# An attention and feed-forward kernel on one core: three moves in the order of its loads, casts and fills

## The chip, the cores and the metric

The kernel runs on one core of one Trainium2 chip. The metric is the device time of one execution in microseconds (us). The kernel before the change took 229.86 us, the median of three runs (228.38, 229.86 and 230.62).

## What is computed

Two stages follow each other. The first is attention for 4 batches of 8 heads, 768 positions, head size 64. Three heads (0, 2, 6, "retrieval") look at all earlier positions; the other five ("stream") look at the first 4 positions and at a window of 64. The second stage is a feed-forward layer over the 3072 tokens, with a leaky slope of its own for each hidden unit:

```
scores = q @ k.T / sqrt(64)                  # masked: causal, or sinks and window
a = exp(scores - max) / sum
x = (a @ v) as [3072, 512]                   # heads side by side
h = x @ w_in                                 # 512 -> 2048
out = (max(h, 0) + alpha * min(h, 0)) @ w_out    # 2048 -> 512
```

All inputs are float32; the kernel works in bfloat16 with float32 sums.

## The kernel before

The heads go in pairs: (2, 6), (1, 5), (0, 4), (3, 7). With 4 batches there are 16 segments, n = 0 to 15; segment n holds pair n % 4 of batch n // 4. Segments 0 to 3 are batch 0, 4 to 7 batch 1. For each segment the kernel loads queries, keys and values, casts them to bfloat16, brings queries and keys into transposed form, multiplies keys by queries (scores), takes the exponent, multiplies by the values, divides by the sums and transposes the result into `xT`. The feed-forward layer takes a batch's 768 tokens in two groups (t even: 512 tokens, t odd: 256), multiplies them by w_in in 16 blocks of 128 hidden units and then by w_out.

Nothing decides the order at run time. A list written out by hand, `ORDER` (lines 14 to 71), names some 1,076 steps, and the kernel emits them one by one (lines 809 to 812). Each engine works through its own instructions in that order, so a step's place in the list sets what stands ahead of it on its engine and, for loads, on its queue. The names in the list that matter here:

- `Lq5`, `Lk3`, `Lv3`: the loads of segment 5's queries, segment 3's keys and values. All go out on SyncE's queue (SP). `Lq` is one DMA (line 209), `Lk` two (line 223), `Lv` two for the two heads (line 246) and, for each stream head of batch 0, one more for the last 24 rows (line 248). Four buffers each (`qf`, `kf`, `vf`) are used in turn: `Lq5` writes the buffer that `Cq1` read. SP's loads share eight semaphores in turn, so each load waits for the landing of the one eight before it.
- `Cq5`, `Ck3.0`, `Ck3.1`, `Cv2`: casts to bfloat16. Strings at lines 298 to 300 say which engine does them; for `Cq5`, `Ck3`, `Cv2` it is GpSimd (POOL). After `Cv` come small copies that repeat the first four rows for stream heads (line 308).
- `Tq5`, `tq5`: six transposes on TensorE (line 365) into a PSUM bank, and the copy out of it, here on ScalarE (line 370). `Tk`, `tk` are the same for keys.
- `S`, `s`: scores on TensorE (lines 415 and 432, masks at 464 and 503) and their exponent on ScalarE. `A`, `a`: the product with the values (line 554) and the division on VectorE. `X`, `x`: transposing the result (line 579) and copying it to `xT`.
- `wi0` to `wi7`: the loads of w_in, issued by POOL with a cast on the way (line 694). A pair, such as `wi0` and `wi1`, brings 512 of the 2048 columns. `wo0` to `wo3` are those of w_out (line 698).
- `P0.5.1`: group 0, hidden block 5, second part of the product with w_in (line 599); `p` and `g` are what ScalarE and VectorE make of it. `O`, `o`: the product with w_out (line 619) and its way out.
- `vz0` to `vz3`: VectorE fills the last slot of a value buffer with zeros (`vf[i][:, 6]`, line 710), which `Lv` then writes in part: the 24-row load of `Lv3` (line 248) waits for `vz3`. `kfz0` to `kfz3` are the same for keys on POOL (line 740).
- `warm`: TensorE products of zeros that keep it at work (line 689).

PSUM has eight banks. A step that needs one takes the one given back longest ago among those that it may use (`take`, line 144), so moving a step can change which bank it gets and whose release it waits for.

Before the change, SP's loads stand in the order Lk3, Lv1, Lq3, Lv2, Lq5, Lv3, Lk4, Lk5, Lk7, Lk6, Lq4, Lq6, and POOL's steps in the order Cv0, wi1, kfz0, Ck3.1, wi0, Ck3.0, Cq3, Cv1, Cv2, nz1, wi6, wi7, Cq5, wi5, wi4, kfz2, Cv3.0, wi2, Ck4.0, Ck4.1, kfz3, nr, Ck5.0, wi3, ns, kfz1, Ck5.1, wo0 to wo3, Cq4. Here `nz1` is a fill, `nr` and `ns` build masks.

Of the kernel before, what the change touches and what calls it, by code (L numbers as in the profile page):

```python
# [13 lines left out]
ORDER = """  # L14
busy zero La id warm0 kz3 Lq0.0 sz1 vz2 nms nmr so1 vz0 Lq0.1 Lk1 warm8 warm5 warm3 kz1 qz0 one Lq1 Lk0 Ck0.0 kz2
Cq0.0 Tq0.0 tq0.0 Tk0.0 qz warm2 Lk2 kz0 tk0.0 Ck1.0 Ck1.1 Cq0.1 Tk1 S0.0.1 s0.0.1 Tq0.1 S0.0.0 Cq1 warm7 Lv0 tk1.0
sz2 vz1 Tq1 Lq2 Ck0.1 S0.0.2 s0.0.0 tk1.1 Tk0.1 Ck2.1 tq1 S1.1.0 s0.0.2 Ck2.0 warm4 tq0.1 nz0 s1.1.0 Cq2 tk0.1 Cv0 Lk3
S0.1.0 wi1 kfz0 Lv1 vo ro0 Ck3.1 s0.1.0 Lq3 wi0 Ck3.0 Cq3 sz0 idf S1.0.0 so2 Al s1.0.0 so0 al S0.1.1 s0.1.1 Lv2 Tq2
Tk2 tk2.1 tk2.0 S0.1.2 Lq5 S1.0.1 A0.0 s0.1.2 a0.0 Cv1 A0.1 a0.1 Cv2 s1.0.1 tq2 S1.1.1 nz1 Tk3 S2.0.1 tk3.0 s1.1.1 vz3
S2.0.2 X0 s2.0.1 x0 wi6 s2.0.2 wi7 Lv3 Cq5 Tq3 tk3.1 S2.0.0 wi5 m4.0.2 warm6 S2.1.0 A1.0 a1.0 Lk4 s2.0.0 A2.0 S2.1.1  # L20
A1.1 a2.0 tq3 s2.1.0 a1.1 S3.0.0 s2.1.1 s3.0.0 A2.1 a2.1 S3.1.1 X1 S3.0.1 s3.0.1 Lk5 wi4 kfz2 Cv3.0 Lk7 wi2 X2 Tq5
Ck4.0 s3.1.1 S3.1.0 tq5 x1 P0.0.0 x2 P0.0.1 A3.0 P0.1.0 P0.1.1 Lk6 Lq4 Lq6 Ck4.1 kfz3 nr Cv3.1 s3.1.0 A3.1 Lv7 Lv5 Lq7
Ck5.0 wi3 a3.0 P0.2.0 P0.3.0 P0.3.1 a3.1 X3 x3 ns kfz1 P0.2.1 Tk4 near2 P1.2 P0.1.2 P0.2.2 P0.0.2 p1.2 p0.1 g0.1 Ck5.1
P1.0 P0.3.2 g1.2 P0.15 tk4.0 p0.2 g0.2 p0.15 wo0 p1.0 Lk8 near0 g0.15 g1.0 ro1 P1.12 P1.14 m12.1.2 p0.0 g0.0 wo1 tk4.1
p1.12 P0.14 g1.12 p0.14 g0.14 P0.13 p0.13 g0.13 P0.11 p1.14 Tk5 Ck7.1 g1.14 P1.10 tk5.0 p0.11 p1.10 Ck6.0 Ck7.0 g0.11
m8.0.2 tk5.1 wo2 Lv6 Lv4 P0.10 P0.8 p0.8 Tk7 g1.10 wo3 Cq4 Lk9 P0.12 P1.8 p0.10 g0.8 p0.12 g0.10 Tq4 P0.6 P0.9 p0.3
Ck6.1 g0.3 tq4 P0.4.0 P0.5.0 Tk6 P0.4.1 p1.8 g1.8 tk7.0 p0.9 g0.9 Cq6 P0.5.1 P0.5.2 p0.5 g0.12 p0.6 tk6.1 P0.4.2 g0.6
g0.5 tk6.0 S4.0.5 P0.7 p0.7 P1.6 g0.7 P1.4 s4.0.5 p0.4 Tq6 m4.1.2 tk7.1 g0.4 Cv5 p1.6 g1.6 O0.1.0 tq6 S4.0.3 O0.2.0
O0.2.1 S5.1.1 S5.0.0 S4.0.1 S6.1.0 m14.0.2 p1.4 g1.4 s5.0.0 O0.1.1 s4.0.3 s4.0.1 O0.2.2 S5.0.2 S5.1.0 S4.0.2 S5.1.2
s6.1.0 m4.0.1 Cv7 O0.3.0 s5.0.2 s5.1.2 s5.1.1 s4.0.2 O0.1.2 s5.1.0 O0.1.3 o0.1 Cq7 Cv4 O0.3.1 m5.1.0 m8.1.2 m5.0.2  # L30
m4.0.3 m5.1.2 S4.0.0 S4.1.4 S5.0.1 S4.0.4 S4.1.0 s4.0.4 s5.0.1 Lk10 m5.0.1 O0.2.3 O0.3.2 Tq7 m5.0.0 o0.2 s4.1.0 m4.0.4
m5.1.1 A5.1 s4.0.0 m4.0.0 a5.1 O0.3.3 tq7 S7.0.0 S7.0.1 S4.1.3 S7.1.1 S6.0.5 S4.1.1 m4.0.5 s4.1.4 o0.3 Lq9 s4.1.3 Ck8
m4.1.3 A5.0 a5.0 X5 s4.1.1 A4.0 s7.0.0 s7.1.1 Lk11 Lq8 s7.0.1 a4.0 s6.0.5 near1 m7.0.0 m7.1.1 m4.1.0 O1.1.0 S7.1.0
S6.0.4 S7.0.2 S4.1.5 S6.0.1 S7.1.2 S6.1.1 O1.1.1 Cv6 s7.1.0 O1.0.0 s4.1.5 m7.0.1 s6.1.1 m4.1.5 m6.1.1 s7.1.2 m6.1.0
s7.0.2 m7.0.2 S6.0.2 S4.1.2 S6.1.2 S6.0.0 s6.0.4 s4.1.2 s6.0.1 s6.1.2 O1.0.1 m6.0.5 m7.1.0 m4.1.1 m4.1.4 m7.1.2 m6.1.2
S6.0.3 A4.1 s6.0.0 m6.0.0 m6.0.1 A7.1 O1.1.2 A6.1 s6.0.3 m6.0.4 m6.0.3 s6.0.2 a4.1 a6.1 A6.0 A7.0 a6.0 O1.1.3 O0.0.0
O0.0.1 O0.0.2 O1.0.2 m10.0.2 O1.0.3 O0.0.3 o0.0 X4 X6 a7.1 a7.0 X7 P2.9 P2.3 p2.9 P3.4 Ck9 Cq9 g2.9 P2.14 p2.14 g2.14
Cq8 p3.4 Lq10 Lq11 Dk8.0 P2.10 p2.10 Dk9.1 o1.0 p2.3 g2.3 g3.4 Dk8.1 P3.2 P3.14 P3.12 P2.8 Dq8 P2.1 P3.8 o1.1 p3.2
Dk9.0 Lv10 g2.10 Dq9 p3.14 P2.7 Ck10 g3.2 p3.12 g3.12 g3.14 P2.2 p2.2 g2.2 Cq10 Dq10 P2.11 p2.1 g2.1 p2.11 p2.8 g2.11
P3.6 P2.5 p2.5 g2.5 P2.13 p2.13 g2.8 g2.13 P2.0 p2.0 g2.0 p2.7 P3.0 p3.0 P2.4 S8.0.5 Lv8 Lv11 P2.15 P2.12 s8.0.5 Cq11  # L40
g3.0 p2.15 g2.7 g2.15 S8.0.0 p2.12 g2.12 Ck11 p3.6 S9.0.2 P2.6 p2.6 g3.6 s8.0.0 p2.4 g2.4 g2.6 s9.0.2 p3.8 P3.10 g3.8
p3.10 O3.0.0 O2.0.0 S8.1.5 s8.1.5 O3.0.1 O2.0.1 g3.10 m8.0.0 Cv8 S8.1.3 S9.0.0 S8.0.3 S9.1.1 S8.0.1 S9.1.0 s8.1.3
s9.1.0 s8.0.1 s9.0.0 s8.0.3 m8.0.3 m8.0.1 O2.0.2 O2.0.3 o2.0 Dk10.1 Lv9 m9.0.0 Cv9 m8.0.5 Dk11.0 m9.1.0 m9.0.2 S8.0.4
S9.0.1 S10.1.1 S8.1.4 Dq11 s8.1.4 Lq13 Lk13 O3.0.2 Dk10.0 s9.1.1 s10.1.1 s9.0.1 s8.0.4 O3.0.3 o3.0 Dk11.1 S10.1.0
S10.1.2 m9.0.1 S11.0.2 S9.1.2 S8.0.2 S11.0.0 s9.1.2 Cv10 m9.1.1 A9.0 s11.0.2 s10.1.0 O2.3.0 m9.1.2 A9.1 a9.0 a9.1 X9
# [804 lines left out]
```

## Time and profile before

| what | us |
|---|---|
| median of three runs | 229.86 |
| the profiled execution | 230.9 |
| its span (first to last instruction) | 229.2 |
| TensorE busy (97% of the span) | 222.5 |
| VectorE busy | 150.6 |
| ScalarE busy | 140.8 |
| GpSimd busy | 46.0 |

The profile is one execution. Its span leaves out what lies before the first and after the last instruction, here 1.7 us. The granted TensorE clock is full in all slices of the page. The DMA engines are busy from 2 us to about 150 us; they move 37.26 MB, most of it (27.60 MB) for SP's queue and 8.93 MB for POOL's. The start of the program, until 28 us, is attention for batch 0 alone; from 28.07 us on TensorE also multiplies by w_in. Times in the text count from the span's start.

### The profile page before, as it was taken

The page shows a single profiled execution, that of the slowest core. Times are in us where ns is not written, and L with a number is a line of the kernel's source. Part 1 is how long each engine was busy: PE and PEld are TensorE (multiplying, and loading weights), DVE is VectorE, ACT ScalarE, POOL GpSimd, SP SyncE. Part 2 cuts the span into 40 slices and gives each one's busy share as a digit, 9 for nine tenths or more (in the row PEclk, how much of TensorE's full clock was granted, in tenths as well). Part 3 has the DMA queues.
Part 4 walks back from the last instruction along what each step waited for, and adds up shares of the span by engine and source line. Part 5 has one row for each costly group of instructions (what it writes and reads, how often), then busy time and mean ns, then how long its engine had stood idle before and what let it go on. Part 6 is the DMA issues. An engine that isn't in the chain of part 4 may idle for free.

```text
span 229.2 us, 5248 instructions
## 1 busy us (share of the span) xinstructions
PE 222.5 (97%) x2005; PEld 136.1 (59%) x2005; DVE 150.6 (66%) x394; ACT 140.8 (61%) x285; POOL 46.0 (20%) x91
## 2 busy tenths in 40 slices
PE   8997999999999999999999999999999999999994
PEld 8887966654455656555456455556556555664454
DVE  5779749975479915899699209986586635966000
ACT  3889529999799127477995127787594236563311
POOL 6775998100230001000400001000110110000000
PEclk9999999999999999999999999999999999999999
DMA  6999999999997799999969799995821420000213
GB/s 196 307 231 214 249 228 270 206 196 210 212 264 166 131 198 215 191 149 193 247 167 216 174 272 152 204 185 99 138 93 38 115 94 0 0 4 0 92 72 112
DMA packets 94957, 37.26 MB, mean 163 GB/s; under 512 B 81980, under 2 KB 93140, under 8 KB 94932
## 3 DMA queue, kind: packets, MB, share of 16 engines
q1 hardware_dynamic: 88676, 27.60, 60.9%
q0 software_dynamic: 5792, 8.93, 17.7%
q10 hardware_dynamic: 464, 0.40, 0.5%
q8 instruction: 15, 0.25, 0.5%
q14 instruction: 10, 0.08, 0.1%
HBM read 27.58 MB, written 6.29 MB: 148 GB/s over the span
## 4 chain that ended last, share of the span: by engine, by line
PE 87%; DMA 3%; ACT 3%; DVE 3%; SPq 1%; issue 1%; POOL 0%; DVEq 0%; POOLq 0%
PE P L599 35%; PE P L619 33%; PE P L554 7%; PE P L432 4%; DMA vf<-in_v_dram 3%; PE P L689 3%; PE P L638 2%; ACT neg L604 1%; PE P L365 1%; DVE kT L394 1%; PE P L579 1%; DVE eS L530 1%; PE P L425 1%; ACT kT L394 1%; PE P L415 1%
## 5 line engine op out<-in xcount | busy, mean ns | idle before, releaser
L611 DVE SCALAR_TENSOR_TENSOR g<-neg,oma,P 128x256 bf16<-128x256 f32 (+1 forms) x128 | 71.0, 608 | 36.1 <-ACT neg L604 35.6
L599 PE MATMUL P<-xT,w_in_b 128*128 128x512 bf16 (+1 forms) x512 | 86.3, 326 | 0.0
L619 PE MATMUL P<-w_out_b,g 128*128 128x512 bf16 x368 | 85.4, 379 | 0.0
L604 ACT ACTIVATE neg<-P 128x512 f32<-128x512 f32 x96 | 54.1, 599 | 29.5 <-PE P L599 25.1
L599 PEld LDWEIGHTS <-w_in_b 128*128 128x128 bf16 x512 | 49.5, 98 | 31.9 <-DVE g L611 0.2
L619 PEld LDWEIGHTS <-g 128*128 128x128 bf16 x368 | 33.7, 98 | 37.3 <-issue 1.2
L471 ACT ACTIVATE eR<-P 128x448 bf16<-128x448 f32 (+4 forms) x63 | 37.0, 634 | 5.4 <-PE P L432 2.5
L625 ACT COPY ot<-P 128x512 f32<-128x512 f32 x23 | 13.8, 601 | 37.7 <-PE P L619 32.9
L629 POOL DMA_DIRECT2D out_dram<-ot x18 | 10.3, 571 | 112.9 <-ACT ot L625 112.7
L519 ACT ACTIVATE eS<-P 128x352 bf16<-128x352 f32 x45 | 20.9, 491 | 3.7 <-PE P L432 3.7
L565 DVE TENSOR_TENSOR xn<-P,rcp 128x448 bf16<-128x448 f32 (+1 forms) x32 | 19.4, 608 | 1.1
L530 DVE TENSOR_TENSOR eS<-eS,ms_near 128x352 bf16<-128x352 bf16 x45 | 15.0, 351 | 4.4 <-ACT eS L519 4.2
L481 DVE TENSOR_TENSOR eR<-eR,mr_near 128x128 bf16<-128x128 bf16 (+5 forms) x54 | 10.7, 225 | 4.0 <-ACT eR L471 4.0
L432 PE MATMUL P<-qT,kT 64*128 64x176 bf16 (+13 forms) x181 | 11.7, 251 | 0.3 <-DVE g L611 0.3
L564 DVE RECIPROCAL rcp<-P 128x7 f32<-128x7 f32 (+1 forms) x32 | 6.3, 197 | 8.5 <-PE P L554 8.4
L432 PEld LDWEIGHTS <-kT 64*128 64x128 bf16 x181 | 7.2, 94 | 7.6 <-issue 6.4
L415 PE MATMUL P<-qT,kT 128*128 128x192 bf16 (+14 forms) x68 | 11.3, 251 | 0.2 <-ACT eS L525 0.2
L554 PE MATMUL P<-vb,eS 128*128 128x65 bf16 x260 | 11.0, 193 | 0.4 <-DVE eS L530 0.4
L554 PEld LDWEIGHTS <-eS 128*128 128x128 bf16 x260 | 9.7, 97 | 2.9 <-DVE eS L530 0.6
L554 PE MATMUL P<-vb,eR 128*128 128x65 bf16 x276 | 10.1, 193 | 1.2 <-POOL vb L350 1.2
L554 PEld LDWEIGHTS <-eR 128*128 128x128 bf16 x276 | 9.5, 97 | 2.4 <-issue 1.3
L647 DVE COPY ot<-P 128x128 f32<-128x128 f32 x1 | 0.3, 292 | 14.3 <-PE P L638 14.3
(96 smaller groups left out, 177.4 us busy)
## 6 DMA issues: line engine op xcount, KB each, us to landing
out_dram<-ot POOLq DMA_DIRECT2D x18, 256.0 KB, 3.6
kf<-in_k_dram SPq DMA_DIRECT2D x21, 192.0 KB
qf<-in_q_dram SPq DMA_DIRECT2D x18, 192.0 KB
vf<-in_v_dram SPq DMA_DIRECT2D x17, 192.0 KB
vf<-in_v_dram SPq DMA_DIRECT2D x14, 196.0 KB
qf<-in_q_dram SPq DMA_DIRECT2D x7, 384.0 KB
w_in_b<-in_moe_w_in_dram POOLq DMA_DIRECT2D x8, 256.0 KB, 9.0
w_out_b<-in_moe_w_out_dram POOLq DMA_DIRECT2D x4, 512.0 KB, 13.4
```

The lines of the kernel that those rows point to most:

```text
L415: nc.tensor.matmul(to, keys, queries, start=True, stop=stop)
L432: nc.tensor.matmul(to, keys[own], queries[own], start=True, stop=True)
L471: nc.scalar.activation(ebuf[n, hh][:, lo:hi].rearrange("p (x c) -> p x c", x=len(parts)), P[:, got[0]:got[0] + len(parts), 0:(hi - lo) // ...
L519: nc.scalar.activation(slots, sc[:, 0:352].rearrange("p (s c) -> p s c", c=176), AF.Exp, scale=scale)
L530: nc.vector.tensor_tensor(slots, slots, ms_near[:, 0:2, :] if m == 0 else ms_near[:, 1:3, :], op=ALU.mult)
L554: nc.tensor.matmul(pav[:, i, :], e[:, o:o + 128], vv[:, j, hh, 0:D + 1], start=(m == 0), stop=(m == len(terms) - 1))
L565: nc.vector.tensor_tensor(xn[n][:, 0:nt, D * hh:D * hh + D], pav[:, :, 0:D], rcp.to_broadcast([128, nt, D]), op=ALU.mult)
L599: nc.tensor.matmul(psg[:, w * i:w * (i + 1)], w_in_b[:, c, 128 * fb:128 * (fb + 1)], xT[:, c, o:o + w], start=(x == 0), stop=(x == 3))
L604: nc.scalar.activation(neg[t, f], bank(held["P", t, f][0]), AF.Relu, scale=-1.0)
L611: nc.vector.scalar_tensor_tensor(g_buf[t % 2][:, fb, 0:w], neg[t, f][:, c], oma[:, fb:fb + 1], bank(got[0])[:, c], op0=ALU.mult, op1=ALU.add)
L619: nc.tensor.matmul(bank(held["O", t, s][0]), g_buf[t % 2][:, f, 128 * s:128 * (s + 1)], w_out_b[:, f, :], start=(f == 0), stop=(f == 15))
L625: nc.scalar.copy(ot, bank(got[0]))
```

## The change

Only `ORDER` changes. Four things move, and no step is added or removed:

- `wi1` and `wi0`, the first two loads of w_in on POOL, go behind `Ck3.1` and `Ck3.0`, the casts of the last pair's keys. POOL's order becomes Cv0, kfz0, Ck3.1, Ck3.0, wi1, wi0, Cq3.
- `vz3`, a fill on VectorE, goes from ahead of `x0` to right behind `vz1`, ahead of `tk1.1`.
- `Lq5`, the load of batch 1's second pair of queries, goes on SP's queue from ahead of `Lv3` to behind it.
- What follows from that load goes later too: `Cq5` on POOL from ahead of wi5 to behind Cv3.0, `Tq5` on TensorE and `tq5` on ScalarE from ahead of `S3.1.0` (Tq5) and right behind it (tq5) to behind `P0.1.1`.

The lines of the list that differ in more than where they break, from line 17 on, with those after:

```diff
-sz2 vz1 Tq1 Lq2 Ck0.1 S0.0.2 s0.0.0 tk1.1 Tk0.1 Ck2.1 tq1 S1.1.0 s0.0.2 Ck2.0 warm4 tq0.1 nz0 s1.1.0 Cq2 tk0.1 Cv0 Lk3
-S0.1.0 wi1 kfz0 Lv1 vo ro0 Ck3.1 s0.1.0 Lq3 wi0 Ck3.0 Cq3 sz0 idf S1.0.0 so2 Al s1.0.0 so0 al S0.1.1 s0.1.1 Lv2 Tq2
-Tk2 tk2.1 tk2.0 S0.1.2 Lq5 S1.0.1 A0.0 s0.1.2 a0.0 Cv1 A0.1 a0.1 Cv2 s1.0.1 tq2 S1.1.1 nz1 Tk3 S2.0.1 tk3.0 s1.1.1 vz3
-S2.0.2 X0 s2.0.1 x0 wi6 s2.0.2 wi7 Lv3 Cq5 Tq3 tk3.1 S2.0.0 wi5 m4.0.2 warm6 S2.1.0 A1.0 a1.0 Lk4 s2.0.0 A2.0 S2.1.1
-A1.1 a2.0 tq3 s2.1.0 a1.1 S3.0.0 s2.1.1 s3.0.0 A2.1 a2.1 S3.1.1 X1 S3.0.1 s3.0.1 Lk5 wi4 kfz2 Cv3.0 Lk7 wi2 X2 Tq5
-Ck4.0 s3.1.1 S3.1.0 tq5 x1 P0.0.0 x2 P0.0.1 A3.0 P0.1.0 P0.1.1 Lk6 Lq4 Lq6 Ck4.1 kfz3 nr Cv3.1 s3.1.0 A3.1 Lv7 Lv5 Lq7
...
+sz2 vz1 vz3 Tq1 Lq2 Ck0.1 S0.0.2 s0.0.0 tk1.1 Tk0.1 Ck2.1 tq1 S1.1.0 s0.0.2 Ck2.0 warm4 tq0.1 nz0 s1.1.0 Cq2 tk0.1 Cv0
+Lk3 S0.1.0 kfz0 Lv1 vo ro0 Ck3.1 s0.1.0 Lq3 Ck3.0 wi1 wi0 Cq3 sz0 idf S1.0.0 so2 Al s1.0.0 so0 al S0.1.1 s0.1.1 Lv2
+Tq2 Tk2 tk2.1 tk2.0 S0.1.2 S1.0.1 A0.0 s0.1.2 a0.0 Cv1 A0.1 a0.1 Cv2 s1.0.1 tq2 S1.1.1 nz1 Tk3 S2.0.1 tk3.0 s1.1.1
+S2.0.2 X0 s2.0.1 x0 wi6 s2.0.2 wi7 Lv3 Lq5 Tq3 tk3.1 S2.0.0 wi5 m4.0.2 warm6 S2.1.0 A1.0 a1.0 Lk4 s2.0.0 A2.0 S2.1.1
+A1.1 a2.0 tq3 s2.1.0 a1.1 S3.0.0 s2.1.1 s3.0.0 A2.1 a2.1 S3.1.1 X1 S3.0.1 s3.0.1 Lk5 wi4 kfz2 Cv3.0 Cq5 Lk7 wi2 X2
+Ck4.0 s3.1.1 S3.1.0 x1 P0.0.0 x2 P0.0.1 A3.0 P0.1.0 P0.1.1 Tq5 tq5 Lk6 Lq4 Lq6 Ck4.1 kfz3 nr Cv3.1 s3.1.0 A3.1 Lv7 Lv5
...
```

More of the change, by code (lines that the diff above doesn't have):

```diff
@@ L21 @@
-A1.1 a2.0 tq3 s2.1.0 a1.1 S3.0.0 s2.1.1 s3.0.0 A2.1 a2.1 S3.1.1 X1 S3.0.1 s3.0.1 Lk5 wi4 kfz2 Cv3.0 Lk7 wi2 X2 Tq5
-Ck4.0 s3.1.1 S3.1.0 tq5 x1 P0.0.0 x2 P0.0.1 A3.0 P0.1.0 P0.1.1 Lk6 Lq4 Lq6 Ck4.1 kfz3 nr Cv3.1 s3.1.0 A3.1 Lv7 Lv5 Lq7
-Ck5.0 wi3 a3.0 P0.2.0 P0.3.0 P0.3.1 a3.1 X3 x3 ns kfz1 P0.2.1 Tk4 near2 P1.2 P0.1.2 P0.2.2 P0.0.2 p1.2 p0.1 g0.1 Ck5.1
-P1.0 P0.3.2 g1.2 P0.15 tk4.0 p0.2 g0.2 p0.15 wo0 p1.0 Lk8 near0 g0.15 g1.0 ro1 P1.12 P1.14 m12.1.2 p0.0 g0.0 wo1 tk4.1
-p1.12 P0.14 g1.12 p0.14 g0.14 P0.13 p0.13 g0.13 P0.11 p1.14 Tk5 Ck7.1 g1.14 P1.10 tk5.0 p0.11 p1.10 Ck6.0 Ck7.0 g0.11
@@ L26 @@
[L26 to L40, printed above, removed]
@@ L41 @@
-g3.0 p2.15 g2.7 g2.15 S8.0.0 p2.12 g2.12 Ck11 p3.6 S9.0.2 P2.6 p2.6 g3.6 s8.0.0 p2.4 g2.4 g2.6 s9.0.2 p3.8 P3.10 g3.8
-p3.10 O3.0.0 O2.0.0 S8.1.5 s8.1.5 O3.0.1 O2.0.1 g3.10 m8.0.0 Cv8 S8.1.3 S9.0.0 S8.0.3 S9.1.1 S8.0.1 S9.1.0 s8.1.3
+sz2 vz1 vz3 Tq1 Lq2 Ck0.1 S0.0.2 s0.0.0 tk1.1 Tk0.1 Ck2.1 tq1 S1.1.0 s0.0.2 Ck2.0 warm4 tq0.1 nz0 s1.1.0 Cq2 tk0.1 Cv0
+Lk3 S0.1.0 kfz0 Lv1 vo ro0 Ck3.1 s0.1.0 Lq3 Ck3.0 wi1 wi0 Cq3 sz0 idf S1.0.0 so2 Al s1.0.0 so0 al S0.1.1 s0.1.1 Lv2
+Tq2 Tk2 tk2.1 tk2.0 S0.1.2 S1.0.1 A0.0 s0.1.2 a0.0 Cv1 A0.1 a0.1 Cv2 s1.0.1 tq2 S1.1.1 nz1 Tk3 S2.0.1 tk3.0 s1.1.1
@@ new lines @@
+S2.0.2 X0 s2.0.1 x0 wi6 s2.0.2 wi7 Lv3 Lq5 Tq3 tk3.1 S2.0.0 wi5 m4.0.2 warm6 S2.1.0 A1.0 a1.0 Lk4 s2.0.0 A2.0 S2.1.1
+A1.1 a2.0 tq3 s2.1.0 a1.1 S3.0.0 s2.1.1 s3.0.0 A2.1 a2.1 S3.1.1 X1 S3.0.1 s3.0.1 Lk5 wi4 kfz2 Cv3.0 Cq5 Lk7 wi2 X2
+Ck4.0 s3.1.1 S3.1.0 x1 P0.0.0 x2 P0.0.1 A3.0 P0.1.0 P0.1.1 Tq5 tq5 Lk6 Lq4 Lq6 Ck4.1 kfz3 nr Cv3.1 s3.1.0 A3.1 Lv7 Lv5
+Lq7 Ck5.0 wi3 a3.0 P0.2.0 P0.3.0 P0.3.1 a3.1 X3 x3 ns kfz1 P0.2.1 Tk4 near2 P1.2 P0.1.2 P0.2.2 P0.0.2 p1.2 p0.1 g0.1
+Ck5.1 P1.0 P0.3.2 g1.2 P0.15 tk4.0 p0.2 g0.2 p0.15 wo0 p1.0 Lk8 near0 g0.15 g1.0 ro1 P1.12 P1.14 m12.1.2 p0.0 g0.0 wo1
@@ new lines @@
+tk4.1 p1.12 P0.14 g1.12 p0.14 g0.14 P0.13 p0.13 g0.13 P0.11 p1.14 Tk5 Ck7.1 g1.14 P1.10 tk5.0 p0.11 p1.10 Ck6.0 Ck7.0
+g0.11 m8.0.2 tk5.1 wo2 Lv6 Lv4 P0.10 P0.8 p0.8 Tk7 g1.10 wo3 Cq4 Lk9 P0.12 P1.8 p0.10 g0.8 p0.12 g0.10 Tq4 P0.6 P0.9
+p0.3 Ck6.1 g0.3 tq4 P0.4.0 P0.5.0 Tk6 P0.4.1 p1.8 g1.8 tk7.0 p0.9 g0.9 Cq6 P0.5.1 P0.5.2 p0.5 g0.12 p0.6 tk6.1 P0.4.2
+g0.6 g0.5 tk6.0 S4.0.5 P0.7 p0.7 P1.6 g0.7 P1.4 s4.0.5 p0.4 Tq6 m4.1.2 tk7.1 g0.4 Cv5 p1.6 g1.6 O0.1.0 tq6 S4.0.3
+O0.2.0 O0.2.1 S5.1.1 S5.0.0 S4.0.1 S6.1.0 m14.0.2 p1.4 g1.4 s5.0.0 O0.1.1 s4.0.3 s4.0.1 O0.2.2 S5.0.2 S5.1.0 S4.0.2
@@ new lines @@
+S5.1.2 s6.1.0 m4.0.1 Cv7 O0.3.0 s5.0.2 s5.1.2 s5.1.1 s4.0.2 O0.1.2 s5.1.0 O0.1.3 o0.1 Cq7 Cv4 O0.3.1 m5.1.0 m8.1.2
+m5.0.2 m4.0.3 m5.1.2 S4.0.0 S4.1.4 S5.0.1 S4.0.4 S4.1.0 s4.0.4 s5.0.1 Lk10 m5.0.1 O0.2.3 O0.3.2 Tq7 m5.0.0 o0.2 s4.1.0
+m4.0.4 m5.1.1 A5.1 s4.0.0 m4.0.0 a5.1 O0.3.3 tq7 S7.0.0 S7.0.1 S4.1.3 S7.1.1 S6.0.5 S4.1.1 m4.0.5 s4.1.4 o0.3 Lq9
+s4.1.3 Ck8 m4.1.3 A5.0 a5.0 X5 s4.1.1 A4.0 s7.0.0 s7.1.1 Lk11 Lq8 s7.0.1 a4.0 s6.0.5 near1 m7.0.0 m7.1.1 m4.1.0 O1.1.0
+S7.1.0 S6.0.4 S7.0.2 S4.1.5 S6.0.1 S7.1.2 S6.1.1 O1.1.1 Cv6 s7.1.0 O1.0.0 s4.1.5 m7.0.1 s6.1.1 m4.1.5 m6.1.1 s7.1.2
@@ new lines @@
+m6.1.0 s7.0.2 m7.0.2 S6.0.2 S4.1.2 S6.1.2 S6.0.0 s6.0.4 s4.1.2 s6.0.1 s6.1.2 O1.0.1 m6.0.5 m7.1.0 m4.1.1 m4.1.4 m7.1.2
+m6.1.2 S6.0.3 A4.1 s6.0.0 m6.0.0 m6.0.1 A7.1 O1.1.2 A6.1 s6.0.3 m6.0.4 m6.0.3 s6.0.2 a4.1 a6.1 A6.0 A7.0 a6.0 O1.1.3
+O0.0.0 O0.0.1 O0.0.2 O1.0.2 m10.0.2 O1.0.3 O0.0.3 o0.0 X4 X6 a7.1 a7.0 X7 P2.9 P2.3 p2.9 P3.4 Ck9 Cq9 g2.9 P2.14 p2.14
+g2.14 Cq8 p3.4 Lq10 Lq11 Dk8.0 P2.10 p2.10 Dk9.1 o1.0 p2.3 g2.3 g3.4 Dk8.1 P3.2 P3.14 P3.12 P2.8 Dq8 P2.1 P3.8 o1.1
+p3.2 Dk9.0 Lv10 g2.10 Dq9 p3.14 P2.7 Ck10 g3.2 p3.12 g3.12 g3.14 P2.2 p2.2 g2.2 Cq10 Dq10 P2.11 p2.1 g2.1 p2.11 p2.8
@@ L43 @@
+g2.11 P3.6 P2.5 p2.5 g2.5 P2.13 p2.13 g2.8 g2.13 P2.0 p2.0 g2.0 p2.7 P3.0 p3.0 P2.4 S8.0.5 Lv8 Lv11 P2.15 P2.12 s8.0.5
+Cq11 g3.0 p2.15 g2.7 g2.15 S8.0.0 p2.12 g2.12 Ck11 p3.6 S9.0.2 P2.6 p2.6 g3.6 s8.0.0 p2.4 g2.4 g2.6 s9.0.2 p3.8 P3.10
+g3.8 p3.10 O3.0.0 O2.0.0 S8.1.5 s8.1.5 O3.0.1 O2.0.1 g3.10 m8.0.0 Cv8 S8.1.3 S9.0.0 S8.0.3 S9.1.1 S8.0.1 S9.1.0 s8.1.3
 s9.1.0 s8.0.1 s9.0.0 s8.0.3 m8.0.3 m8.0.1 O2.0.2 O2.0.3 o2.0 Dk10.1 Lv9 m9.0.0 Cv9 m8.0.5 Dk11.0 m9.1.0 m9.0.2 S8.0.4
```

## The prediction

> **What bounds the kernel now.** I read the page first, then TensorE's waits, then the chain, then the timelines around the one wait that stands out.
>
> ```profile
> PE 222.5 (97%) x2005; PEld 136.1 (59%) x2005; DVE 150.6 (66%) x394; ACT 140.8 (61%) x285; POOL 46.0 (20%) x91
> ```
> TensorE (PE) is the bound: 6.7 us of the span of 229.2 are idle, so no reordering can bring more. The list of what PE waited for, whole span, us in total, times, longest:
>
> ```profile
> PE P L554 <- POOL vb L350: 1.2, 1, 1.2
> PE P L689 <- DVE zero L290: 1.1, 1, 1.1
> PE P L554 <- DVE eS L530: 0.4, 1, 0.4
> PE P L365 <- DVE kT L396: 0.3, 1, 0.3
> ```
> The 1.1 is the start of the program. One wait is left that a change of order can reach: the first row, A2.0's matmuls for the values that Cv2 casts on POOL. PE's timeline there:
>
> ```profile
> 21.22 0.55 PE L554 MATMUL P<-vb,eS 128*128 128x65 bf16 x13
> 22.94 0.97 PE L554 MATMUL P<-vb,eR 128*128 128x65 bf16 x27 [1.17 <-POOL vb L350]
> ```
> POOL's timeline (start, duration, what it waited for):
>
> ```profile
> 14.67 0.78 POOL L694 DMA_DIRECT2D w_in_b<-in_moe_w_in_dram  x1
> 15.44 0.23 POOL L290 MEMSET kf<- 128x128 f32 x1
> 15.59 0.52 POOL L330 CAST g<-kf 128x384 bf16<-128x384 f32 x1
> 16.03 0.64 POOL L694 DMA_DIRECT2D w_in_b<-in_moe_w_in_dram  x1
> 16.65 0.53 POOL L330 CAST g<-kf 128x384 bf16<-128x384 f32 x1
> 17.26 0.83 POOL L317 CAST g<-qf 128x768 bf16<-128x768 f32 x1
> ...
> 19.03 0.63 POOL L308 COPY vb<-vb 4x192 f32<-4x192 f32 x2
> 21.95 0.93 POOL L350 CAST vb<-vf 128x896 bf16<-128x896 f32 x1 [2.29 <-DMA vf<-in_v_dram]
> ```
> POOL was free for Cv2 at 19.66 and sat until 21.95 for a load. The chain names it:
>
> ```profile
> 14.35 7.49 DMA vf<-in_v_dram
> ```
> This is the second of Lv2's loads (196 KB), 7.49 us from issue to landing. A load's semaphore counts 16 landings, one per DMA engine. In the trace 15 of them come at 18.18 to 19.08, the sixteenth at 21.84: one engine is late and alone holds Cv2. What came between is seen in the DMA view by queue (packets, MB, share of 16 engines; q1 is SP's, q0 POOL's), first for 17.0 to 17.5, then for 18.0 to 18.5:
>
> ```profile
> q1 hardware_dynamic: 523, 0.13, 120.1%
> q0 software_dynamic: 1, 0.00, 1.2%
> ```
>
> ```profile
> q0 software_dynamic: 51, 0.05, 93.9%
> q1 hardware_dynamic: 48, 0.01, 12.9%
> ```
> The first w_in packet starts at 17.46. The late engine landed Lv2's previous load at 18.03, so it had all of this load's 768/16 = 48 packets of 256 B before it when w_in's 1 KB packets came in between. A 256 B packet takes 18 ns alone and 31 beside w_in, a w_in packet 96.
>
> **The change, part by part.**
>
> *wi1, wi0 behind Ck3.* No instruction is added. On POOL kfz0 and both Ck3 casts (kf3 landed before 14.4) move ahead of wi1: its issue goes from 14.67 by 0.15 + 0.44 + 0.61 (start to start in the rows above) to 15.87, wi0's from 16.03 to 15.87 + 0.77 = 16.64. Cq3 still starts at 17.26. With the same 2.79 us from issue to first packet, w_in comes at 18.66 instead of 17.46. Alone, the late engine's 48 packets end at 18.03 + 48 x 0.018 = 18.9; if w_in's 16 packets of wi1 get among the last of them, at 18.9 + 16 x 0.096 = 20.4. The bounds are 18.9 and the old 21.84 (w_in comes no later on that engine than before); I take 20.4 or earlier, because 1.2 us is more than the 0.87 that the 48 packets need. Cv2 then starts between 19.66 and 20.5, ends 0.99 later (21.95 to PE's 22.94), by 21.5. PE reaches A2.0 at 22.94 - 1.17 = 21.77: the 1.17 goes. What is late next: nothing on POOL, as Cv3.0, Ck4 and so on were queued behind Cv2 and come 1.5 to 2.3 earlier. wi0 and wi1 landed at 24.83 at the latest; 1.2 later is 26.0, and P0.0.0 needs them at 28.07 - 1.0 - 0.34 (Tq5 no longer ahead of it) = 26.7: hidden, with 0.7 to spare.
>
> The Trainium skill (DMA: Bandwidth & Descriptors, Latency and other measured facts) gives about 1 us to the first byte of a GpSimd DMA. The rows say 2.79 for wi1 and 2.02 for wi6 (24.08 to 26.10). By the page's figure, as an estimate, w_in would be there at 16.9, ahead of all 48 packets; the stall would stay and the sum be zero.
>
> *vz3 nearer the front.* On DVE it now runs behind vz1 (9.56), ahead of tk1.1. Memsets there start 0.19 to 0.20 apart; the old place at 19.88 took 0.09. PE waits there for DVE (the 0.3 row, Tk0.1 behind tk1.1) and is full from 13.9 to 21.7, so the delay passes on: cost 0.09 to 0.20, I take 0.15. In return SP's queue is free of this:
>
> ```profile
> 15.55 0.37 SPq L209 DMA_DIRECT2D qf<-in_q_dram  x1
> 15.96 0.74 SPq L246 DMA_DIRECT2D vf<-in_v_dram  x1
> 20.07 0.33 SPq L248 DMA_DIRECT2D vf<-in_v_dram  x1
> ```
> Lv3's third line stood 3.3 us for vz3 (19.88), with two more Lv3 loads and Lk4, Lk5, Lk7, Lk6, Lq4 behind it. Now Lv3's four loads issue at 15.5 to 17.5. That does not speed PE by itself: SP's loads share eight semaphores, each waits for the one eight before it, and from 16 us on the engines are busy all the time, so bytes only change places. Zero, bounds -0.3 to +0.3 (the smaller PE waits of 0.29 and 0.4 further on).
>
> *Lq5, Cq5, Tq5, tq5 later.* Lq5 (issued 15.55, landed 23.13) moves past Lv3's four loads to about 17.5. They hold 1584 packets of 256 B; Lq5 lands 1 to 3 us later, 24 to 26. Cq5 (0.83) moves on POOL past wi5, wi4, kfz2 and Cv3.0, and would start at about 25.5 to 27. On PE Tq5's six transposes (0.34) move behind P0.1.1; the same work, reached at 27.06 - 1.0 + 2.3 = 28.4, so 0.6 or more behind Cq5's end. Tq5 takes another PSUM bank, freed by s3.1.1 long before. tq5 (0.79 on ACT) moves into the 4.15 us that ACT waited before 33.3. Cv3.0 gains: its sink copies ended at 28.43 and A3.0 came at 28.71. Sum zero; cover for Tq5 gone only if Lq5 lands past 27.5.
>
> *Later due times.* PE is about 1 us earlier at everything that loads feed. The tightest I found is Tq4:
>
> ```profile
> 43.12 0.83 POOL L317 CAST natq<-qf 128x768 bf16<-128x768 f32 x1 [3.80 <-DMA qf<-in_q_dram]
> ```
>
> ```profile
> 45.04 0.50 PE L365 MATMUL P<-ident,natq 128*128 128x128 bf16 x6
> ```
> Lq4 landed at 43.07, Cq4 ended at 43.95, Tq4 came at 45.04. One us earlier it comes at 44.02, 0.07 behind. If Lq4 keeps its time, nothing is lost. Its landing is bounded by the fifteen other engines' 40.42 and, for w_in and w_out packets that come 1 to 2 us earlier among the loads, by about 45.6; I take the old time.
>
> **Sum.** -1.17 + 0.15 = -1.0. The profiled execution took 230.9 (span 229.2), so it would take 229.9 (span 228.2). It lies 1.04 above the median of the runs, 229.86; from there -1.0 is 228.8.
>
> **Rivals.**
> *The load stays late* (the change does not do what it says). For it: only landings, not single engines, are seen before 18; and if w_in came 0.6 us earlier than worked out, all 48 packets would meet the 32 of wi1 and wi0: 18.9 + 32 x 0.096 = 22.0. Against: fifteen landings by 19.08, the sixteenth with wi1's last at 21.80. Then A2.0 starts at 22.94 as before, vz3's 0.15 vanishes in that wait: 229.9.
> *Lq4 takes the place* (the other side). POOL's w_in and w_out issues come earlier, and where both queues have packets they pass one for one (68 against 68 between 34.0 and 34.5), so SP's small packets lose; from 23.5 to 26.1 q0 had been empty and q1 caught up. PE stands at Tq4 for the landing + 0.95 - 44.02 (0.05 and 0.83 for Cq4, 0.07 on to PE as at A2.0). It eats the gain when Lq4 lands after 44.1, 1 us later than now; at 45.6 it costs 2.5, 1.5 net: 231.4. Against: SP issues Lv3 3.3 us earlier.
> *The smaller waits go too*: with the loads ahead, 0.29 at 55.99 and 0.4 at 65.6 vanish: 228.8 - 0.7 = 228.1.
>
> The skill (same page, Queues, rings and completion order) has each engine go round robin between queues by the packet, which the 68 against 68 bear out; it speaks against any gain from order alone: a w_in issued later only stands among other loads. By that alone the sum would be zero.
>
> **How the numbers follow.** Forecast 228.8: 0.50, its own range 228.2 to 229.5. Late load, 229.9: 0.20. Lq4 or another load late, 230 to 231.4 and rarely more: 0.20. Smaller waits too, 228.1: 0.10. The range 227.9 to 231.2 leaves out about 0.2. A change of 1% (2.3 us) is about the least that a measurement of this kernel can tell from none. Below 227.6 needs twice the stall that can go: 0.06. Above 232.2 needs Lq4 or a w_in load over 3 us late: 0.08. Within: 0.86.
>
> **What would show it.** Right: no wait <-POOL vb L350 in PE's list, Cv2 starting by 20.9 on POOL, A2.0 at about 21.9, first w_in packet near 18.7, the L248 of Lv3 issued before 17. The 0.3 before Tk0.1 grown by 0.1 to 0.2. Wrong: Cv2 still at 21.9 (first rival), PE idle before an L365 on natq or natm (second), or before the first L599 for w_in.

## The result and the profile after

| | before | after |
|---|---|---|
| median of 22 runs each, us | 230.39 (228.38 to 232.37) | 231.22 (230.56 to 232.07) |
| span of the first profiled execution, us | 229.2 | 229.8 |

The changed kernel is slower: the ratio of the times is 1.0048, with a 95% interval of 1.0029 to 1.0066. The forecast was 228.8; the time lies 0.02 us above the upper end of the range (231.2), on the side that was given to the second rival. The prediction took 1% for about the least that can be told from nothing; half of that is clear of it here, and it goes the other way, for a cause that the prediction did not name. Of the runs beside the experiments, eleven took 233.4 us or more with a granted TensorE clock of 0.983 to 0.993, and the medians and ratios below leave them out.

The first view is the busy time by engine, after.

```profile
PE 221.8 (97%) x2005; PEld 135.1 (59%) x2005; DVE 148.9 (65%) x394; ACT 140.6 (61%) x285; POOL 45.9 (20%) x91
```

The work is the same, so the difference is again idle time of TensorE. The list of what PE waited for, after (us in total, times, longest):

```profile
PE P L554 <- ACT eS L525: 1.6, 1, 1.6
PE P L689 <- DVE zero L290: 1.1, 1, 1.1
PE P L365 <- POOL g L317: 0.6, 1, 0.6
PE P L365 <- DVE kT L396: 0.5, 1, 0.5
```

The row that the prediction was about, `<-POOL vb L350` with 1.2 us, is gone. In its place stands a larger one that was not there before: 1.6 us for an exponent from ScalarE. The 0.6 (line 317) is a wait at 14.94 for Cq2, whose load Lq2 came later than before; of the four moves only vz3 stands ahead of it, and a second execution, shown further on, does not have it. PE's timeline shows the places, first before (A3.1), then after (A2.0, Tq5, A3.1):

```profile
29.75 0.56 PE L554 MATMUL P<-vb,eS 128*128 128x65 bf16 x13
```

```profile
22.02 0.97 PE L554 MATMUL P<-vb,eR 128*128 128x65 bf16 x27
...
28.84 0.50 PE L365 MATMUL P<-ident,natq 128*128 128x128 bf16 x6
30.94 0.57 PE L554 MATMUL P<-vb,eS 128*128 128x65 bf16 x13 [1.60 <-ACT eS L525]
```

A2.0 (22.02) starts without a wait, 0.92 us earlier than before. The six transposes of Tq5 (28.84) now stand directly ahead of A3.1, and A3.1 stands idle for 1.60 us after them. POOL's timeline, after, answers to the one of before:

```profile
16.74 1.41 POOL L694 DMA_DIRECT2D w_in_b<-in_moe_w_in_dram  x2
18.14 0.85 POOL L317 CAST g<-qf 128x768 bf16<-128x768 f32 x1
...
19.92 0.63 POOL L308 COPY vb<-vb 4x192 f32<-4x192 f32 x2
20.51 0.92 POOL L350 CAST vb<-vf 128x896 bf16<-128x896 f32 x1
```

Cv2 (20.51) no longer sits for its load: Lv2's second load had all its sixteen landings between 19.17 and 19.45, where before the last came at 21.84. So the mechanism that the change was worked out on is there. The new wait is explained by ScalarE's timeline, first before, then after (start, duration, what was done, what it waited for):

```profile
26.87 0.87 ACT L525 ACTIVATE eS<-P 128x384 bf16<-128x384 f32 x2 [0.66 <-PE P L503]
27.63 0.81 ACT L370 COPY qT<-P 128x768 bf16<-128x768 bf16 x1
28.30 0.84 ACT L525 ACTIVATE eS<-P 128x768 bf16<-128x768 f32 x1
```

```profile
25.95 0.87 ACT L525 ACTIVATE eS<-P 128x384 bf16<-128x384 f32 x2 [0.65 <-PE P L503]
29.37 0.80 ACT L370 COPY qT<-P 128x768 bf16<-128x768 bf16 x1 [2.55 <-PE P L365]
30.07 0.82 ACT L525 ACTIVATE eS<-P 128x768 bf16<-128x768 f32 x1
```

The order of these three lines is the same in both kernels: the exponents s3.1.1, then tq5 (the copy of the transposed queries), then the exponent s3.1.0. In the list, `tq5` stood ahead of `s3.1.0` before the change and still does. What changed is when tq5 can run: Tq5 went behind P0.1.1 on TensorE, so ScalarE sits 2.55 us for it, and s3.1.0, whose scores PE had finished by 27.32, starts behind it at 30.07. A3.1 needs s3.1.0, so TensorE sits as well.

How far TensorE is behind or ahead of the kernel before, by the starts of the same instructions in the two traces: 0.92 ahead at A2.0 and 0.92 ahead at P0.0.0 (27.15 against 28.07), 1.19 behind at A3.1 (30.94 against 29.75), 0.6 behind from 68 us to the end. The last step down is a wait that the kernel before had near 65 us (0.4 for the masked exponents, line 530) and that this execution did not have.

### The profile page after: what moved, and what is told of

It reads as the page before. It is cut to its first block, busy times and chain, and to the rows that moved or that the text cites. A ratio compares the mean times of both kernels' runs of the same rounds, so it can differ in the third digit from the quotient of the medians.

```text
span 229.8 us, 5247 instructions
## 1 busy us (share of the span) xinstructions
PE 221.8 (97%) x2005; PEld 135.1 (59%) x2005; DVE 148.9 (65%) x394; ACT 140.6 (61%) x285; POOL 45.9 (20%) x91
## 4 chain that ended last, share of the span: by engine, by line
PE 88%; ACT 3%; DMA 2%; issue 2%; SPq 1%; POOL 1%; DVE 0%; POOLq 0%; DVEq 0%; ACTq 0%
PE P L599 35%; PE P L619 34%; PE P L554 7%; PE P L432 4%; DMA kf<-in_k_dram 2%; PE P L365 2%; PE P L415 2%; PE P L638 2%; ACT neg L604 1%; PE P L503 1%; SPq L223 1%; PE P L579 1%; PE P L425 1%; ACT kT L394 1%; ACT eS L525 1%
## 5 line engine op out<-in xcount | busy, mean ns | idle before, releaser
L530 DVE TENSOR_TENSOR eS<-eS,ms_near 128x352 bf16<-128x352 bf16 x45 | 14.5, 338 | 5.0 <-ACT eS L519 4.9
```

The source lines that it names most:

```text
L530: nc.vector.tensor_tensor(slots, slots, ms_near[:, 0:2, :] if m == 0 else ms_near[:, 1:3, :], op=ALU.mult)
```

## The experiments

The experiments are called e1 to e12 below, by the numbers in their names: e1 moved the exponent ahead, e2 only w_in, e3 only Tq5 and tq5, e4 the whole group of the queries, e5 only vz3, e6 w_in and vz3, e7 Tq5 a little later, e8 vz3 in a gap, e9 Lq4 ahead of the keys; e10 and e11 are the kernel before and e12 the changed one, profiled again.

Theory: the 1.6 us come from s3.1.0 standing behind tq5 on ScalarE. Rivals: they come with the later Lq5 and Cq5, or with the moves of w_in and vz3, or it is an accident of one execution. A second question came up with the first runs: why so little of the 1.17 us at A2.0 shows in the times. The ratios are to the kernel before, run beside each group of kernels; the last three are single profiled executions.

**The exponent ahead of the transposes.** The changed kernel, with one step moved so that it stands ahead of tq5 on ScalarE:

```diff
-... A3.0 P0.1.0 P0.1.1 Tq5 tq5 Lk6 Lq4 Lq6 Ck4.1 kfz3 nr Cv3.1 s3.1.0 A3.1 Lv7 Lv5
+... A3.0 P0.1.0 P0.1.1 s3.1.0 Tq5 tq5 Lk6 Lq4 Lq6 Ck4.1 kfz3 nr Cv3.1 A3.1 Lv7 Lv5
```

> The changed kernel with one step moved: s3.1.0, the exponent of the last scores of batch 0, goes on ScalarE ahead of tq5, the copy of segment 5's queries, instead of behind it. Theory (the copy in the way): s3.1.0 stood behind tq5, which stood for Tq5 on TensorE until 29.3; A3.1 then waits no more, its 1.60 us in TensorE's list are gone, and with the small wait ahead of it 1.6 to 1.8 us go: ratio to the kernel before 0.996 to 0.998, about 229.5. Rival (late loads): the wait is not what costs, since loads that come late stop TensorE at the next place, Tq4 on Cq4; then the 1.6 us come back there and the ratio stays at 1.003 to 1.006.

Measured: 229.78 us (12 runs) against 230.25, ratio 0.9981 [0.9959, 1.0004]. The interval does not meet that of the changed kernel, 1.0029 to 1.0066. PE's waits in it:

```profile
PE P L689 <- DVE zero L290: 1.1, 1, 1.1
PE P L653 <- DVE eS L290: 0.7, 1, 0.7
PE P L365 <- DVE kT L396: 0.5, 1, 0.5
...
PE P L554 <- DVE vb L308: 0.2, 1, 0.2
```

The 1.6 is gone, and ScalarE's timeline has the two steps the other way round:

```profile
27.86 0.81 ACT L525 ACTIVATE eS<-P 128x768 bf16<-128x768 f32 x1 [0.53 <-PE P L503]
29.88 0.80 ACT L370 COPY qT<-P 128x768 bf16<-128x768 bf16 x1 [1.21 <-PE P L365]
```

One step put elsewhere takes back the whole loss. The 0.7 (L653) and the 0.2 (L308) are told of in the last section; the first, at 14.84, stands ahead of the step that was moved.

**Only Tq5 and tq5 moved.** The kernel before, with Lq5, Cq5, w_in and vz3 where they were:

```diff
-... Lk7 wi2 X2 Tq5
-Ck4.0 s3.1.1 S3.1.0 tq5 x1 P0.0.0 x2 P0.0.1 A3.0 P0.1.0 P0.1.1 Lk6 ...
+... Lk7 wi2 X2
+Ck4.0 s3.1.1 S3.1.0 x1 P0.0.0 x2 P0.0.1 A3.0 P0.1.0 P0.1.1 Tq5 tq5 Lk6 ...
```

> The kernel before with Tq5 and tq5 alone moved behind P0.1.1; Lq5 and Cq5 keep their places. Theory (the copy in the way): s3.1.0 stands behind tq5 on ScalarE and A3.1 waits 1.5 to 2 us for it, though no load is any later; the whole is 1.2 to 2 us slower, ratio 1.005 to 1.009. Rival (late loads): without a later load there is no wait, ratio 0.998 to 1.002.

Measured: 231.86 (7 runs), ratio 1.0077 [1.0049, 1.0104], a loss of 1.8 us by itself. PE's waits:

```profile
PE P L554 <- ACT eS L525: 1.6, 1, 1.6
PE P L554 <- POOL vb L350: 1.2, 1, 1.2
```

Both stalls stand in one execution, and no load was moved: the new one does not come from the loads' order.

**The whole group of the queries moved.** The kernel before, with Lq5, Cq5, Tq5 and tq5 at their new places:

```diff
-... S0.1.2 Lq5 S1.0.1 ...   wi7 Lv3 Cq5 Tq3 ...   Cv3.0 Lk7 wi2 X2 Tq5 ...   S3.1.0 tq5 x1 ...   P0.1.1 Lk6
+... S0.1.2 S1.0.1 ...   wi7 Lv3 Lq5 Tq3 ...   Cv3.0 Cq5 Lk7 wi2 X2 ...   S3.1.0 x1 ...   P0.1.1 Tq5 tq5 Lk6
```

> The kernel before with Lq5, Cq5, Tq5 and tq5 moved as in the change; w_in and vz3 keep their places. Theory (the copy in the way): as with Tq5 and tq5 alone, ratio 1.005 to 1.009, and what Lq5 and Cq5 add or take is under 0.3 us. Rival (late loads): Lq5 behind Lv3, which here still stands for vz3 until 20, lands later still; Cq5 is late, Tq5 itself waits, and the ratio is over 1.009.

Measured: 232.56 (9 runs), ratio 1.0109 [1.0065, 1.0154]. PE's waits begin with

```profile
PE P L554 <- ACT eS L525: 1.6, 1, 1.6
PE P L689 <- DVE zero L290: 1.1, 1, 1.1
PE P L415 <- ACT qT L370: 0.8, 2, 0.5
PE P L554 <- POOL vb L350: 0.7, 1, 0.7
```

The 1.6 again. The ratio is in the range that the expectation gave to its rival (over 1.009), but what that rival said did not come: Tq5 did not wait for Cq5. That the group costs more than Tq5 alone is not shown: the intervals overlap, and the 0.8 (two waits, at 7.83 and 10.95) lies ahead of everything that was moved.

**Tq5 a little later only.** The changed kernel, with Tq5 and tq5 behind P0.0.0 instead of P0.1.1:

```diff
-... x1 P0.0.0 x2 P0.0.1 A3.0 P0.1.0 P0.1.1 Tq5 tq5 Lk6 ...
+... x1 P0.0.0 Tq5 tq5 x2 P0.0.1 A3.0 P0.1.0 P0.1.1 Lk6 ...
```

> The changed kernel with Tq5 and tq5 moved 1.26 us of TensorE's work nearer the front, behind P0.0.0; tq5 stays ahead of s3.1.0 on ScalarE. Theory (the copy in the way): P0.0.1, A3.0, P0.1.0 and P0.1.1 (0.22 + 0.39 + 0.43 + 0.22 us) now run while tq5 and s3.1.0 do, so A3.1's wait shrinks from 1.60 to about 0.3 us: ratio 0.997 to 1.001, some 1.2 us under the changed kernel. Rival (late loads): nothing of the loads changes, so the ratio stays at 1.003 to 1.006, or Tq5 itself waits for Cq5.

Measured: 230.50 (12 runs) against 229.98, ratio 1.0033 [1.0002, 1.0063]. PE's waits for the exponent at A3.1 and for the value copies behind it:

```profile
PE P L554 <- ACT eS L525: 0.3, 1, 0.3
...
PE P L554 <- DVE vb L308: 0.3, 1, 0.3
```

The wait follows the place of Tq5, 0.3 from 1.6, as the theory had it. The time does not: the ratio is in the rival's range (1.003 to 1.006), and it is not shown to be under that of the changed kernel, as the intervals overlap. Why the time did not follow the wait stays open.

**Only w_in moved.** The kernel before, with wi1 and wi0 behind Ck3.0:

```diff
-S0.1.0 wi1 kfz0 Lv1 vo ro0 Ck3.1 s0.1.0 Lq3 wi0 Ck3.0 Cq3 ...
+S0.1.0 kfz0 Lv1 vo ro0 Ck3.1 s0.1.0 Lq3 Ck3.0 wi1 wi0 Cq3 ...
```

> The kernel before with wi1 and wi0 alone moved behind Ck3.0. Theory: the second load of Lv2 lands by 20.5 or so, the 1.2 us wait of A2.0 goes, ratio 0.994 to 0.998. Rival (loads only change places): w_in's packets come later among other loads and something else waits as long, ratio 0.999 to 1.002.

Measured: 230.19 (12 runs), ratio 0.9992 [0.9964, 1.002], the rival's range. Lv2's second load landed complete at 19.43, and A2.0 did not wait, as the theory had it. PE's list still has 0.6 for line 350, but that is another place, A4.0 in batch 1, for a late Lv4:

```profile
21.63 0.97 PE L554 MATMUL P<-vb,eR 128*128 128x65 bf16 x27
...
67.14 0.79 PE L554 MATMUL P<-vb,eR 128*128 128x65 bf16 x21 [0.59 <-POOL vb L350]
```

POOL's timeline around Cv2:

```profile
17.91 0.83 POOL L317 CAST g<-qf 128x768 bf16<-128x768 f32 x1 [0.77 <-DMA qf<-in_q_dram]
...
20.26 0.92 POOL L350 CAST vb<-vf 128x896 bf16<-128x896 f32 x1
```

Cq3 sat 0.77 us for its load Lq3, and Cv1 and Cv2 came behind it on POOL; Cv2 (20.26) was still early enough. So the stall at A2.0 went with this move alone, and the time is not shown to be any shorter. In the profiled execution TensorE was 1.30 us ahead of the first profile of the kernel before at A3.1 and 0.76 at the end.

**Only vz3 moved.** The kernel before, with `vz3` behind `vz1`:

```diff
-sz2 vz1 Tq1 ...   s1.1.1 vz3
+sz2 vz1 vz3 Tq1 ...   s1.1.1
```

> The kernel before with vz3 alone moved behind vz1. Theory: VectorE is 0.15 us later at the keys of segment 1, TensorE's wait for them grows from 0.3 to 0.45 us, and A2.0 still waits for Cv2, which takes that up; SP no longer stands for vz3 until 20, but no wait of TensorE hangs on that: ratio 0.998 to 1.003. Rival (loads ahead help): with Lv3 and what is behind it 3.3 us earlier, waits further on go and the ratio is under 0.998.

Measured: 229.86 (12 runs), ratio 0.9983 [0.995, 1.0016]. A2.0 waited 0.5 in the profiled execution, with w_in where it was; thirteen landings of Lv2's second load came by 18.46 and three at 20.67 to 20.87.

**w_in and vz3 moved, the queries not.** The two edits above together:

```diff
-sz2 vz1 Tq1 ...   Lk3 S0.1.0 wi1 kfz0 ...   Lq3 wi0 Ck3.0 Cq3 ...   s1.1.1 vz3
+sz2 vz1 vz3 Tq1 ...   Lk3 S0.1.0 kfz0 ...   Lq3 Ck3.0 wi1 wi0 Cq3 ...   s1.1.1
```

> The kernel before with wi1, wi0 and vz3 moved, and everything of segment 5's queries at its old place. Theory (the copy in the way): without the moved copy there is no 1.6 us wait, A2.0's wait goes, 0.15 us comes for vz3: ratio 0.995 to 0.999, like the changed kernel with s3.1.0 ahead (0.998). Rival (Lq5 behind Lv3 is needed): ahead of Lv3 and with w_in later, Lq5 and Lv3 land later, Cv3.0 is late for A3.0 and the ratio is 1.000 or more.

Measured: 230.0 (12 runs), ratio 0.9997 [0.9969, 1.0024]. The profiled execution took 233.65, so only the place of its wait is read. PE's timeline:

```profile
46.01 0.51 PE L365 MATMUL P<-ident,natq 128*128 128x128 bf16 x6 [2.27 <-POOL natq L317]
```

TensorE was 1.47 us ahead of the first profile of the kernel before and then stood 2.27 us at Tq4, for a late Lq4.

**The zero fill in a gap, and the exponent ahead.** The changed kernel, with s3.1.0 ahead of Tq5 as above, and vz3 behind `al`, where VectorE has time:

```diff
-sz2 vz1 vz3 Tq1 ...   Al s1.0.0 so0 al S0.1.1 ...
+sz2 vz1 Tq1 ...   Al s1.0.0 so0 al vz3 S0.1.1 ...
```

> The changed kernel with s3.1.0 ahead of Tq5 and tq5 (ratio 0.998 by itself) and with vz3 behind al, in a gap that VectorE has from 14.4 to 15.4 us. Theory: TensorE's wait for segment 1's keys falls back from 0.5 to 0.3 us, Lv3 still goes out before 17.5 us: 0.15 us less, ratio 0.995 to 0.998. Rival: the early place of vz3 costs nothing, ratio 0.998 as before or, if Lv3 now lands too late for Cv3.0, above.

Measured: 230.14 (12 runs), ratio 1.0 [0.9974, 1.0025], though the profiled execution has the second shortest span of all, 227.7. Its list has neither a wait for the exponent at A3.1 nor one for vb, and

```profile
PE P L365 <- DVE kT L396: 0.2, 1, 0.2
```

That wait was 0.5 with vz3 right behind vz1, but the ratio is not the theory's 0.995 to 0.998.

**Lq4 ahead of the keys.** The kernel before, with w_in moved, vz3 behind `al`, and Lq4 ahead of Lk7 and Lk6 on SP's queue:

```diff
-... Cv3.0 Lk7 wi2 X2 Tq5 ...   P0.1.1 Lk6 Lq4 Lq6
+... Cv3.0 Lq4 Lk7 wi2 X2 Tq5 ...   P0.1.1 Lk6 Lq6
```

> The kernel before with wi1 and wi0 behind Ck3.0, vz3 behind al (where e8 showed it costs TensorE nothing), the q5 group unmoved, and Lq4 ahead of Lk7 and Lk6 on SP's queue. Theory that a late Lq4 in some executions eats what the early w_in move wins (one profiled execution of e6 had a 2.3 us wait at Tq4): Cq4 never waits long for Lq4 (under 2 us of wait on POOL), no natq wait in TensorE's list, and the median comes 0.5 to 1.0 us under the kernel before, ratio 0.996 to 0.998. Rival, that the stall at A2.0 is in the median execution only some 0.3 us: ratio 0.998 to 1.001, as e2 and e6 had it. Second rival: Lk7 and Lk6, now 384 KB of queries later, make the key transposes wait: over 1.001.

Measured: 230.32 (12 runs) against 230.15, ratio 0.999 [0.9959, 1.0022]. Cq4 no longer waits for its load and A2.0 does not wait, but PE's timeline has

```profile
14.96 0.84 PE L365 MATMUL P<-ident,g 128*128 128x128 bf16 x12 [0.92 <-POOL g L317]
...
43.08 0.51 PE L365 MATMUL P<-ident,natm 128*128 128x128 bf16 x6 [0.59 <-DVE natm L330]
```

1.5 us in other places: for Cq2, ahead of everything that was moved, and for a cast of keys at 43, one of the loads that Lq4 went past. The ratio is the first rival's (0.998 to 1.001); the wait that the second rival named is there, though the ratio is not over 1.001.

**The same kernels profiled again.** The kernel before twice more, the changed one once more, nothing edited.

> The kernel before, unchanged, one more profiled execution. Theory that the stall at A2.0 is different in every execution, and that the first profile (1.17 us, execution 230.9, 0.5 over the median of the kernel's runs) showed a large one: the wait for Cv2's values comes out at another size, 0 to 0.9 us, with a span below 229.2. Rival, that it is the same each time: 1.1 to 1.3 us again.

> The kernel before, unchanged, a further profiled execution. As for the last one: theory, a wait for Cv2's values of 0 to 0.9 us that differs from the other's by over 0.2; rival, 1.1 to 1.3 us again.

> The changed kernel, unchanged, one more profiled execution. Theory that the 1.6 us at A3.1 comes from the order on ScalarE alone and not from a transfer that can be early or late: 1.5 to 1.7 us again at A3.1, less by what TensorE waits between A2.0 and Tq5, and no wait for Cv2's values. Rival, that the 1.6 was an accident of one execution: under 1.0.

PE's timeline in the second and in the third execution of the kernel before, one fence each:

```profile
22.26 0.97 PE L554 MATMUL P<-vb,eR 128*128 128x65 bf16 x27 [0.26 <-POOL vb L350]
...
65.27 0.45 PE L554 MATMUL P<-vb,eS 128*128 128x65 bf16 x9 [0.47 <-DVE eS L530]
```

```profile
21.65 0.97 PE L554 MATMUL P<-vb,eR 128*128 128x65 bf16 x27 [0.32 <-ACT qT L370]
...
44.88 0.51 PE L365 MATMUL P<-ident,natq 128*128 128x128 bf16 x6 [0.97 <-POOL natq L317]
```

And in the second execution of the changed kernel:

```profile
21.57 0.97 PE L554 MATMUL P<-vb,eR 128*128 128x65 bf16 x27
...
30.48 0.57 PE L554 MATMUL P<-vb,eS 128*128 128x65 bf16 x13 [1.60 <-ACT eS L525]
```

The table sets the five executions side by side. Offsets are PE's starts against the first profile of the kernel before, in us, minus is earlier.

| execution | Lv2's last landing | A2.0 waits | offset at A2.0 | at A3.1 | at the end | span |
|---|---|---|---|---|---|---|
| before, first | 21.84 | 1.17 | 0 | 0 | 0 | 229.2 |
| before, second | 21.16 | 0.26 | -0.68 | -0.68 | -0.33 | 228.9 |
| before, third | 20.55 | 0.32 (not for vb) | -1.29 | -1.29 | -0.75 | 228.4 |
| after, first | 19.45 | none | -0.92 | +1.19 | +0.59 | 229.8 |
| after, second | 19.64 | none | -1.37 | +0.74 | +0.25 | 229.4 |

The stall at A3.1 is the same to the last digit in both executions of the changed kernel (1.60), and in e3 and e4: it ends with an instruction's place and not with a landing. The stall at A2.0 ends with a landing and is different in each execution of the kernel before. With e3, e4 and e5, which have w_in at its old place too, the six waits for vb are 1.17, 0.26, 0, 1.17, 0.74 and 0.54, 0.65 on average; the first profile showed the largest, as e3 did. The eight executions with w_in later have none there. In those eight Lv2's second load took 4.13 to 5.63 us from issue to last landing, in the other six 6.10 to 7.49. The theory for both questions held. At the end the changed kernel is on average 0.42 behind, the kernel before 0.36 ahead: 0.78 us apart, as the medians are (0.83).

## Why the prediction was wrong

**The step that failed** is "*tq5 (0.79 on ACT) moves into the 4.15 us that ACT waited before 33.3*", and with it "*Sum zero*" for the queries. It looked for room on ScalarE and for a bank on TensorE, but not for what was queued behind tq5 on ScalarE: s3.1.0, which A3.1 needs. The gap of 4.15 us lies behind s3.1.0; tq5 lies ahead of it. The cost of this one term: from A2.0 to A3.1 it is 6.81 us before (22.94 to 29.75) and 8.92 after (22.02 to 30.94), +2.11, and within 0.01 the same in the further executions of both kernels. Of this 1.60 is the wait, and the rest is Tq5, which now stands in this stretch. Tq5's own time came no cheaper for the move: from A2.0 to P0.0.0 it is 5.13 in both, though six transposes (0.34) had gone from there: S3.1.0, reached that much earlier, now waits for an exponent (0.19 idle at 26.50). The edit alone gave +0.77% in e3, and its undoing (e1) took the changed kernel's loss away. No rival had this mechanism; the time ended near the second rival's 231.4 for another reason.

**The first term, -1.17, was mis-sized.** The mechanism held: first w_in packet at 19.27 and, in the second execution, 18.23 (worked out: near 18.7), Lv2's second load complete at 19.45 and 19.64 (18.9 to 20.4), Cv2 at 20.51 and 20.25 (by 20.5), A2.0 at 22.02 and 21.57 (21.9), no wait there. That the first execution lies so near is in part luck: Cq2's late load put wi1's issue at 16.74 instead of the 15.87 worked out (15.66 in the second). But 1.17 was the stall of one execution. By the offsets at A2.0, the kernel before stood there at -0.66 on average over three executions and the changed one at -1.14 over two: some 0.5 is left of the 1.0. The prediction set its execution 1.04 us above the median of three runs and then took the whole stall off that median, as if the surplus and the stall were different things; as far as three executions tell, part of the 1.04 was the stall itself. With more runs the median before also came out at 230.39 instead of 229.86, so 0.5 us of the miss is the starting point.

**What was won early was partly lost later anyway.** After A3.1 the three executions of the kernel before move by 0, +0.35 and +0.54 to the end: the further ahead they were at 30 us, the more they gave back, at Tq4 for one (0.97 at 44.88 in the third; this is the second rival's place), and in e2 at A4.0 (0.59). In the changed kernel, Tq4 came so late (46.23 in the first) that Lq4, cast at 43.58, was not felt. e2, e5, e6, e8 and e9, each with another load or fill in a better place and without the stall at A3.1, have ratios from 0.9983 to 1.0 with intervals over 1. So the claim that the loads' order brings a full 1 us is not borne out; whether it brings some tenths of a us or nothing stays open, and so does the division between w_in and vz3.

**vz3**: PE's wait for DVE before Tk0.1 went from 0.33 to 0.47 in the first execution, and was 0.29 in the second, against +0.15 worked out. Lv3's first 24-row load was issued at 16.94 and, in the second execution, 15.88 instead of 20.07, as forecast ("before 17"). **Lq5 and Cq5**: in the first execution Cq5 ran 26.14 to 26.96 without a wait, and Tq5 at 28.84 had its operand ready. In the second Cq5 stood 1.33 for Lq5 and ended at 28.07, 0.31 ahead of Tq5 (28.38): this cover held, but by little. **P0.0.0** did not wait for w_in.

**On the two rules that were weighed**: the Trainium skill (DMA: Bandwidth & Descriptors, Latency and other measured facts) gives about 1 us to the first byte. After the change it was 2.5 us from wi1's issue (16.74) to the first w_in packet (19.27), and 2.06 to 3.26 in all fourteen profiled executions, so the measurement decides against that figure here. Three late stores of the output, with little else on the queues, had 1.12 us (issues at 167.11, 169.90 and 183.18 in the first profile of the kernel before). The same page has a round robin between queues (Queues, rings and completion order). By that alone, the prediction said, the change would gain nothing. The view of 34.0 to 34.5 has 77 packets of each queue, not 68, so equal as said; but the queue that was called empty from 23.5 to 26.1 had 8 packets. The late landing did go: 19.45 and 19.64 with w_in later, 20.55 to 21.84 without, and in the first of these w_in's first packet (19.27) came among the load's landings (19.17 to 19.45). That the time did not fall was not shown to come from this rule.

No kernel tried is shown to beat the kernel before. e1 (0.9981, to 1.0004) and e5 (0.9983, to 1.0016) have the lowest ratios.

## What to carry to other kernels

When a step moves later on one engine, look up the step that consumes it on each other engine, and ask what stands behind that consumer in its own queue: ScalarE took its list in order here, and one copy with a late input held the exponent behind it from 27.32 to 30.07. A stall that ended with a transfer's landing differed from execution to execution here (0 to 1.17), one that ended with an instruction's place did not (1.60 each time); profile the kernel two or three times before the first kind is taken off at its full size. And when a profiled execution lies above the median, the stall that is to be removed may be the reason: it can't be taken off the median again.
